# A fused attention unit and token mixer on one core: a square put ahead of the gate, the extra product in full ahead of a group's body, and another order of transposes on SP

## Chip, core and metric

The kernel runs on one core of a Trainium2 chip. The metric is the device time of one execution in microseconds (us), the median of several executions. Five engines run side by side, each through its own list of instructions in order: TensorE (PE in the profile, its weight loads PEld), VectorE (DVE), ScalarE (ACT), GpSimd (POOL) and SyncE (SP), which here only issues transfers. An engine waits on semaphores that other engines or transfers raise.

## Reference

The first stage is a gated attention without a softmax, the second mixes tokens with weights that are made from its own input. In NumPy, with the shapes of this case (8 batches, S = 3200 tokens, D = 256, key width 64):

```python
attn = np.maximum(z @ z.T / S, 0.0) ** 2        # per batch, 3200 x 3200
x = u * (attn @ v)                               # 3200 x 256

wq, wk = x @ w_q, x @ w_k                        # 3200 x 64
W_tok = wq @ wk.T / np.sqrt(64)
mixed = W_tok @ x                                # = wq @ (wk.T @ x) / 8
out = np.maximum(mixed, 0.0) @ w_out             # 3200 x 256
```

`attn` is symmetric, and `W_tok @ x` is computed as `wq @ (wk.T @ x)`, whose inner factor is 64 x 256.

## The kernel before

**Tiles and groups.** The 25 blocks of 128 tokens of a batch make seven groups: six of four blocks (512 tokens) and a last one of a single block. For each of the 8 batches and each group the kernel forms the scores of the group's columns against all blocks, squares them, multiplies them with `v` into two PSUM banks (`acc`), and gates the sum with `u`. A pair of score tiles (128 x 1024) goes through three hands: `scores` (L268) multiplies on PE into one of three rotating PSUM tiles; `first_stage` (L288) clips it at zero into an fp32 tile `g`, on DVE (L293) or ACT (L291); `second_stage` (L298) squares `g` into an fp16 tile `at`, on ACT (L302) or POOL (L304). Since scores are symmetric, many blocks of `at` also serve a later group after a transpose; `second_stage` issues these transposes on SP at once (L321), into tiles `tt`.

**Steps.** The loop of L919 walks through 169 steps. Each computes up to three pairs of scores for later use, squares the three pairs that the step before it clipped (`waiting`), and multiplies a few blocks of the present group with `v` (its body, `second_product`, L423). Scores run two steps ahead of their use (`LAG`). Some pairs of scores are placed ahead of the body (`pairs`, their count is `heading`, L944 to L947), the others between its matmuls (`between_`, placed by `shares`, L863).

**Two lanes.** A body runs with two halves of the PE array side by side: lane LOW contracts rows 0 to 63 into one bank, lane HIGH rows 64 to 127 into the other. Then the lanes change banks, so that each bank gets both halves. `swap_after` (L402) makes PE wait, at that change, for the ends of the matmuls before it.

**Extras.** A step can carry one extra product in its own PSUM tile: a projection of the second stage (`project`, L726), or keys and heads (`keys_and_heads`, L735); the tile comes from the same three rotating ones as the scores. In a step that begins a group, `parts` (L1025 to L1030) is `[extra, banks]`: first halves of the extra, first halves of the body, change, second halves of the extra, change, second halves of the body.

**Gate.** When a group's last step is done, `gate` (L447) reads the two banks: ACT copies the upper one to `gt` (L465), DVE multiplies the lower one with `u` (L466), POOL multiplies `gt` with `u` (L468); a last group of one block has copies on ACT and DVE and an addition and a multiplication on POOL (L458 to L461). The banks are then free for the next group. The result `x_sb` is transposed on SP by `turn_x` (L471) in the next step, after that step's squares and their transposes (L970 to L976).

**Order.** The order on every engine is the order in which the program text issues the instructions; nothing reschedules them. After the loop the last products follow in a fixed order (L1096 to L1140).

Of the kernel before, what the change touches and what calls it, by code (L numbers as in the profile page):

```python
# [10 lines left out]
FP32 = mybir.dt.float32  # L11
RELU = mybir.ActivationFunctionType.Relu
AOP = mybir.AluOpType
# [3 lines left out]
def kernel(  # L17
# [15 lines left out]
    P = 128  # L33
# [40 lines left out]
    def acc_tile(half, name, dtype=FP32):  # L74
# [4 lines left out]
        v0 z00D z01A w10 t0 w2 w1 c0D z10A z11P t1 c1D v1 s0 s1 e0A v2 e1D z20P z21P q0A s2  # L79
        e2D q1A z30P z31P s3 e3A t2 m0 s4 c2D q2A v3 e4D q3P t3 m1 c3D s5 e5A q4A s6 e6D m2  # L80
        s7 e7D
    """
    ctx.enter_context(tc.manual_schedule())

# [213 lines left out]
    def second_stage(p0, g, on_act):  # L298
        at = pat.tile([P, 2 * W], FP16, tag="at", name="at")
        out = at[:].rearrange("p (a w) -> p a w", a=2)  # L300
        if on_act:
            nc.scalar.square(out=out, in_=g[:])  # L302
        else:
            nc.gpsimd.tensor_mul(out=out, in0=g[:], in1=g[:])  # L304
        blocks = []
        for h, (b, gi, tis) in enumerate(tiles[p0 : p0 + 2]):
            for i, ti in enumerate(tis):
                made[b, gi, ti] = (at, h * W + i * widths[gi])
            gj = group_of(tis[0])
            if is_turned(gi, gj):  # L310
                blocks.append((b, gi, gj, tis[0] - starts[gj] // P, 1, h * W, (h + 1) * W))
        if len(blocks) == 2 and blocks[0][:3] == blocks[1][:3] and blocks[1][3] == blocks[0][3] + 1:
            blocks = [blocks[0][:4] + (2, blocks[0][5], blocks[1][6])]
        for b, gi, gj, n0, nn, c0, c1 in blocks:
            if (b, gi, gj) not in turned:
                bufs = {1: 3, 2: 4, 4: 1}[gj - gi]
# [4 lines left out]
            nc.sync.dma_start_transpose(out=out[:, 4 * n0 : 4 * (n0 + nn), :], in_=at[:, c0:c1])  # L321

    accs = {}

# [146 lines left out]
    def turn_x(b, gi):  # L471
        nn = widths[gi] // P
        if gi < LASTG:
            xTs[b, gi] = pxt.tile([P, 4, ND, P], FP16, tag="xT_sb", name="xT_sb")
        else:
            xTs[b, gi] = pxt.tile([P, 1, ND, P], FP16, tag="xTl", name="xTl", bufs=1)
        nc.sync.dma_start_transpose(
            out=xTs[b, gi][:, 0:nn, :, :].rearrange("p n a s -> p (n a) s"),
            in_=xs[b, gi][:, 0:nn, :].rearrange("p n d -> p (n d)"),
        )  # L480
# [392 lines left out]
    def warm(n):  # L873
        if "x" not in begun:
            begun["x"] = acc_tile(1, "sc")
        for _ in range(n):
            nc.tensor.matmul(
                out=begun["x"][:, 0:P], lhsT=zeros[:], rhs=zeros[:], start=True, stop=True
            )

    def opening(order):
        sc, g = {}, {}
        for word in order.split():
            what, n, by = word[0], int(word[1:2]), word[2:]
            if what == "z":
                cast_first(n, int(by[0]), by[1])
            elif what == "t":
                turn_first(n)
            elif what == "c":
                place_first(n, by)  # L890
            elif what == "v":
                load_first_v(*[(0, 4), (12, 6), (18, 7), (4, 8)][n])
            elif what == "s":
                sc[n] = scores(2 * n)
            elif what == "e":
                g[n] = first_stage(2 * n, sc.pop(n), by == "A")
            elif what == "q":
                second_stage(2 * n, g.pop(n), by == "A")
# [17 lines left out]
    across = False  # L916
    left, first_sizes = [], [4, 5, 5, 5]
    gate_pending = False
    while groups:  # L919
        now[0] = k  # L920
        for fn in at_phase.pop(k, []):
# [55 lines left out]
        while asides:  # L977
            asides.pop(0)()

# [38 lines left out]
        if on_lanes:  # L1018
# [13 lines left out]
            emits = []  # L1032
# [4 lines left out]
            cut = len(rows_) // 4  # L1037
            if split:
                emits += both_lanes([bank[:cut] for bank in banks])
            if parts:  # L1040
                across = not across
            for part, ends_ in zip(parts, firsts):
                emits.append((0, lambda ends_=ends_: swap_after(ends_.values())))
                emits += lanes(part, across, True, {})
                if extra and part is extra[0]:
                    emits.append((0, extra[1]))
            if split:
                emits += both_lanes([bank[cut:] for bank in banks])
            at_ = shares(begins, closes, split, len(between_))
            todo = [(x, lambda p0=p0: stage(p0, scores(p0))) for x, p0 in zip(at_, between_)]  # L1050
            for x in acts[1:]:
                todo.append((0.5 - 1e-6, lambda x=x: second_stage(*x)))
            run(emits, todo)
        else:
            assert not is_split(b, gi)
# [11 lines left out]
                    fn()  # L1067
                extra[1]()
            for x in acts[1:]:
                second_stage(*x)  # L1070
            for fn in matmuls[cut:]:
                fn()
        if closes:
# [22 lines left out]
    while to_turn:  # L1096
        turn_x(*to_turn.pop(0))

    def query(gi, o):
        for fn in whole([projections(last, gi, wq2, o)]):  # L1100
            fn()
        projections_out(last, gi, o)

    halves = [(True, nc.sync, 2), (True, nc.sync, 2)]

    psh = ps_tile("hd")
    assert all(kb == last for kb, _ in keyed)
    for fn in whole([heads(last, sum((kgis for _, kgis in keyed), []), psh, stop=False)]):
        fn()
    last_gram(last, LASTG, psg)  # L1110
    g32 = [pg.tile([P, D], FP32, tag="g", name=f"G{cc}") for cc in range(ND)]
    nc.scalar.copy(out=g32[0][:], in_=psg[0])
    nc.vector.tensor_copy(out=g32[1][:], in_=psg[1])
    while len(fillers) > 1:
        mixed = fillers.pop(0)
        proj_out(*mixed, proj(*mixed), [(False, nc.sync, 4)])
    last_heads(last, g32, psh)
    heads_done(last, psh[:, 1, 0:D])
    second = acc_banks("fo")
    proj_half(*fillers[0], second, 0)  # L1120
    query(LASTG - 1, ps_tile("qq")[:, 0, :])
    mixed = [mix(last, 0, db) for db in range(ND)]
    for db in range(ND):
        mix_out(last, 0, db, mixed[db], on_dve=(db == 1))
    proj_half(*fillers[0], second, 1)
    proj_out(*fillers[0], second, halves)
    for db in range(ND):
        mix_out(last, 1, db, mix(last, 1, db))
    query(LASTG, acc_tile(0, "qq")[:, 0:P])
    proj_out(last, 0, proj(last, 0), [(True, nc.sync, 4)])  # L1130
    proj_out(last, 1, proj(last, 1, acc_banks("fo")), halves)
    mix_out(last, 2, 0, mix(last, 2, 0))
    proj_out(last, 2, proj(last, 2), [(True, nc.sync, 4)])
    mix_out(last, 2, 1, mix(last, 2, 1))
    small = acc_banks("mx")
    last_mix(last, small)
    proj_out(last, 3, proj(last, 3), [(True, nc.sync, 4)])
    proj_out(last, 4, proj(last, 4), [(False, nc.sync, 4)])
    proj_out(last, LASTG, proj(last, LASTG), [(False, nc.sync, 1)])
    proj_out(last, 5, proj(last, 5, acc_banks("fo")), [(False, nc.scalar, 2), (True, nc.sync, 2)])  # L1140


# [28 lines left out]
```

## Time and profile before

| | |
|---|---|
| median of 3 executions | 788.06 us (787.47 to 788.28) |
| the profiled execution: its own time | 788.39 us |
| its span, first to last instruction | 786.6 us |
| granted TensorE clock over the span | 0.998 |
| squares on POOL, L304 | 238 of 1.894 us |
| squares on ACT, L302 | 230 of 1.054 us |
| clips on DVE, L293 | 338 of 1.222 us |
| POOL's gate multiply, L468 | 48 of 1.275 us |
| pieces of `at` turned on SP | 162, 5.0 us from issue to landing |

A line of the timeline gives the start in us, the length, the engine, the source line, the operation, the tiles written and read, the shapes, and how many equal instructions in a row were merged (x). Brackets give idle time of the engine ahead of the row and what ended it. Matmul lengths overlap, so the start of one row to the start of the next is the time that PE spent on it.

### The profile page before, as it was taken

The numbers are of one execution on the slowest core, as the hardware profiler recorded it, in microseconds if no ns is written. First come the engines' busy times: TensorE is split into PE (matmuls) and PEld (weight loads), VectorE is DVE, ScalarE is ACT, GpSimd is POOL, SyncE is SP. The second block draws the span as 40 slices with busy tenths as digits, with TensorE's granted clock in tenths as the row PEclk, the third lists the DMA queues.
The fourth block names the chain that finished last, engine by engine and source line by source line (L and its number), as shares of the span: only waits on it lengthen the run. The fifth ranks groups of instructions, "written<-read, shape, count | busy, mean of one in ns | idle before, by whom it ended". The sixth has DMA issues, their size and how long they took to land. (4 is left out here: it accounts for less than half of the span.)

```text
span 786.6 us, 28630 instructions
## 1 busy us (share of the span) xinstructions
PE 770.5 (98%) x12690; PEld 660.9 (84%) x12690; DVE 470.9 (60%) x457; ACT 559.4 (71%) x655; POOL 551.3 (70%) x363
## 2 busy tenths in 40 slices
PE   9999999999999999999999999999999999999996
PEld 6777878887888878889888997898988898988884
DVE  7654666546756567555766557655575646665434
ACT  7666777767768786675867667758696977675464
POOL 7797797667666587765978768885777546866350
PEclk9999999999999999999999999999999999999999
DMA  9999699996999779998799978999589994989626
GB/s 178 179 207 217 124 203 185 194 183 81 245 180 210 175 158 203 195 226 193 171 211 206 236 159 208 200 215 234 123 209 185 244 220 88 198 190 163 159 68 252
DMA packets 276269, 147.06 MB, mean 187 GB/s; under 512 B 252081, under 2 KB 255665, under 8 KB 276145
## 3 DMA queue, kind: packets, MB, share of 16 engines
q1 hardware_dynamic: 275424, 143.33, 88.8%
q0 software_dynamic: 576, 1.64, 1.1%
q8 instruction: 99, 1.62, 0.9%
q14 instruction: 26, 0.20, 0.1%
q10 hardware_dynamic: 144, 0.26, 0.1%
HBM read 59.38 MB, written 26.21 MB: 109 GB/s over the span
## 5 line engine op out<-in xcount | busy, mean ns | idle before, releaser
L293 DVE TENSOR_SCALAR g<-sc 128x1024 f32<-128x1024 f32 x338 | 411.1, 1222 | 260.8 <-PE sc L279 240.4
L337 PE MATMUL acc<-v_sb,at 64*128 64x256 f16 (+1 forms) x7387 | 482.1, 269 | 4.0 <-POOL at L304 1.4
L304 POOL TENSOR_TENSOR at<-g 128x1024 f16<-128x1024 f32 x238 | 445.0, 1894 | 24.2 <-DMA tt<-at 9.0
L337 PEld LDWEIGHTS <-at 64*128 64x128 f16 (+1 forms) x7387 | 388.7, 94 | 68.6 <-PE acc L337 18.1
L302 ACT ACTIVATE at<-g 128x1024 f16<-128x1024 f32 x230 | 237.8, 1054 | 26.8 <-DMA tt<-at 13.2
L468 POOL TENSOR_TENSOR x_sb<-gt,u_sb 128x512 f16<-128x512 f32 x48 | 61.2, 1275 | 181.8 <-ACT gt L465 136.3
L337 PE MATMUL acc<-v_sb,tt 64*128 64x256 f16 (+1 forms) x2540 | 178.5, 269 | 0.0
L279 PE MATMUL sc<-zT 64*128 64x512 f16 (+1 forms) x1104 | 167.6, 344 | 1.4 <-ACT g L291 1.1
L291 ACT ACTIVATE g<-sc 128x1024 f32<-128x1024 f32 x130 | 133.0, 1023 | 37.0 <-PE sc L279 31.7
L337 PEld LDWEIGHTS <-tt 64*128 64x128 f16 (+1 forms) x2540 | 134.8, 94 | 10.2
L279 PEld LDWEIGHTS <-zT 64*128 64x128 f16 x1104 | 60.2, 94 | 9.6 <-issue 3.8
L602 ACT ACTIVATE rt<-mx 128x1024 f16<-128x1024 f32 x47 | 47.8, 1023 | 27.3 <-PE mx L581 25.2
L465 ACT COPY gt<-acc 128x512 f32<-128x512 f32 x48 | 28.1, 585 | 48.6 <-PE acc L337 46.7
L337 PE MATMUL fo<-wo,rt 64*128 64x256 f16 (+1 forms) x688 | 59.5, 269 | 0.8 <-DVE g L293 0.7
L663 ACT ACTIVATE fo<-fo 128x1024 f32<-128x1024 f32 (+2 forms) x44 | 43.6, 998 | 19.8 <-PE fo L337 19.4
L503 ACT CAST qk<-qk 128x512 f16<-128x512 f32 x47 | 27.5, 584 | 40.4 <-PE qk L337 40.1
L337 PE MATMUL qk<-x_sb,kx 64*128 64x256 f16 x368 | 55.1, 269 | 0.9 <-DVE g L293 0.6
L337 PEld LDWEIGHTS <-rt 64*128 64x128 f16 (+1 forms) x688 | 41.3, 94 | 12.8 <-issue 2.4
L466 DVE TENSOR_TENSOR x_sb<-acc,u_sb 128x512 f16<-128x512 f32 x48 | 33.1, 690 | 26.9 <-PE acc L337 24.3
L337 PEld LDWEIGHTS <-kx 64*128 64x128 f16 (+1 forms) x386 | 36.1, 94 | 7.2 <-DMA kx<-qk 0.6
L337 PE MATMUL qk<-xT_sb,wkq 64*128 64x512 f16 (+1 forms) x90 | 31.7, 376 | 0.0
L337 PE MATMUL qk<-xT_sb,wqk 64*128 64x512 f16 (+1 forms) x94 | 30.1, 377 | 0.0
(80 smaller groups left out, 268.5 us busy)
## 6 DMA issues: line engine op xcount, KB each, us to landing
u_sb<-in_u_dram SPq DMA_DIRECT2D x48, 512.0 KB, 5.2
out_dram<-fo SPq DMA_DIRECT2D x45, 512.0 KB, 3.5
piece<-in_v_dram SPq DMA_DIRECT2D x42, 512.0 KB, 4.6
piece<-in_z_dram SPq DMA_DIRECT2D x7, 512.0 KB, 5.8
tt<-at SPq DMA_TRANSPOSE x162, 5.0
piece<-in_z_dram SPq DMA_DIRECT2D x7, 288.0 KB, 5.8
out_dram<-fo SPq DMA_DIRECT2D x5, 256.0 KB, 2.7
u_sb<-in_u_dram SPq DMA_DIRECT2D x8, 128.0 KB, 3.8
```

What stands on the lines that cost most here:

```text
L279: nc.tensor.matmul(out=sc[:, h, at : at + w], lhsT=zT[b][half : half + dqk, ds(z_at(b, h) + ti * P, P)], rhs=zT[b][half : half + dqk, ds(z ...
L291: nc.scalar.activation(out=g[:], in_=sc[:], func=RELU, scale=GSCALE)
L293: nc.vector.tensor_scalar(out=g[:], in0=sc[:], scalar1=0.0, scalar2=GSCALE, op0=AOP.max, op1=AOP.mult)
L302: nc.scalar.square(out=out, in_=g[:])
L304: nc.gpsimd.tensor_mul(out=out, in0=g[:], in1=g[:])
L337: return nc.tensor.matmul(out=self.out, lhsT=self.lhsT(rows), rhs=self.rhs(rows), start=start, stop=stop)
L465: nc.scalar.copy(out=upper[:], in_=accs[1][:])
L466: nc.vector.tensor_mul(out=x[:, 0:n], in0=accs[0][:, 0:n], in1=ug[:, 0:n])
L468: nc.gpsimd.tensor_mul(out=x[:, n : 2 * n], in0=upper[:], in1=ug[:, n : 2 * n])
L503: nc.scalar.copy(out=qks[b, gi][:, 0:gw], in_=out)
L602: nc.scalar.activation(out=out, in_=ps[:], func=RELU)
L663: nc.scalar.mul(out=flat_out[:, sl], in_=part, mul=FINAL_SCALE)
```

## The change

Three things are moved; no matmul and no other operation on data is added or left out.

1. At the end of each group, POOL squares the first of the pairs that the closing step clipped (`staged[0]`) ahead of the gate's own instructions. Before, that square was POOL's first one of the next step, behind the gate multiply. Its transposes are kept back (`ahead`) and issued in the next step.
2. In a step that begins a group with an extra (and whose group isn't the single block run on split lanes), the extra is done in full ahead of the body: its first halves, a change of lanes, its second halves, its output, then the body's two halves with their own change. One pair of scores fewer stands ahead of the body (`heading` falls by two, not by one); two pairs are placed in between, each right in front of one of the two changes of lanes.
3. `second_stage` returns its transposes instead of issuing them. In each step SP now turns `x` first, then the blocks of the first POOL square (`soon`), those of the ACT square, and those of a second POOL square (`late`) only after the body.

The work after the loop is written as a list of words (`ENDING`) that one function reads; its instructions stand in the same order as before.

```diff
@@ second_stage
-        blocks = []
+        blocks, turns = [], []
...
-            nc.sync.dma_start_transpose(out=out[:, 4 * n0 : 4 * (n0 + nn), :], in_=at[:, c0:c1])
+            turns.append(
+                lambda out=out[:, 4 * n0 : 4 * (n0 + nn), :], c0=c0, c1=c1:
+                nc.sync.dma_start_transpose(out=out, in_=at[:, c0:c1])
+            )
+        return turns
...
+    def each(fns):
+        for fn in fns:
+            fn()
@@ the loop over steps
-            heading = heading - bool(keying or projecting) if begins else 1 - bool(mixing)
+            heading = heading - 2 * bool(keying or projecting) if begins else 1 - bool(mixing)
...
-        seconds = [(p0, g, a) for (p0, g), a in zip(waiting, second_on_act)]
+        seconds = [(p0, g, a) for (p0, g), a in zip(waiting, second_on_act) if g is not None]
         acts = [x for x in seconds if x[2]]
-        for x in seconds:
-            if not x[2]:
-                second_stage(*x)
-        for x in acts[:1]:
-            second_stage(*x)
         while to_turn:
             turn_x(*to_turn.pop(0))
+        soon, late = ahead, []
+        for i, x in enumerate([x for x in seconds if not x[2]]):
+            (late if i else soon).extend(second_stage(*x))
+        for x in acts[:1]:
+            each(second_stage(*x))
+        each(soon)
...
+            emits = []
+            apart = extra and begins and not split
+            if apart:
+                turned_ = {}
+                emits += lanes(extra[0], across, False, turned_)
+                first_done = sum(n for n, _ in emits)
+                emits.append((0, lambda: swap_after(turned_.values())))
+                emits += lanes(extra[0], not across, True, {})
+                emits.append((0, extra[1]))
+                parts = [banks]
...
             at_ = shares(begins, closes, split, len(between_))
+            if apart:
+                all_ = sum(n for n, _ in emits)
+                at_ = [(n - 1) / all_ for n in (first_done, halves_, halves_)][: len(between_)]
...
+        each(late)
+        ahead = []
         if closes:
+            if staged:
+                ahead = second_stage(*staged[0], False)
+                staged[0] = (staged[0][0], None)
             gate(b, gi)
...
@@ after the loop
+    ending(ENDING)
```

More of the change, by code (lines that the diff above doesn't have):

```diff
@@ L1039 @@
                 emits += both_lanes([bank[:cut] for bank in banks])
+            halves_ = sum(n for n, _ in emits)
             if parts:
@@ L1044 @@
                 emits += lanes(part, across, True, {})
-                if extra and part is extra[0]:
+                if extra and not apart and part is extra[0]:
                     emits.append((0, extra[1]))
@@ L1069 @@
             for x in acts[1:]:
[L1070 removed]
+                each(second_stage(*x))
             for fn in matmuls[cut:]:
                 fn()
+        each(late)
+        ahead = []
         if closes:
+            if staged:
+                ahead = second_stage(*staged[0], False)
+                staged[0] = (staged[0][0], None)
             gate(b, gi)
@@ L1097 @@
         turn_x(*to_turn.pop(0))
[L1099 to L1140, printed above, removed]
+    assert len(fillers) == 3 and all(kb == last for kb, _ in keyed)
+    ps_, out_, g32 = {}, {}, {}
+    def home(name, where):
+        if where == "a":
+            return acc_banks(name)
+        ps = ps_tile(name)
+        return [ps[:, 0, :], ps[:, 1, :], ps[:].rearrange("p a w -> p (a w)")]
@@ new lines, in ending @@
+    def ending(order):
+        for word in order.split():
+            what, n, more = word[0], int(word[1:2] or 0), word[2:]
+            if what == "H":
+                ps_["hd"] = ps_tile("hd")
+                heads_ = heads(last, sum((kgis for _, kgis in keyed), []), ps_["hd"], stop=False)
+                for fn in whole([heads_]):
+                    fn()
+            elif what == "G":
+                last_gram(last, LASTG, psg)
+            elif what == "g":
+                g32[n] = pg.tile([P, D], FP32, tag="g", name=f"G{n}")
+                (nc.scalar.copy if more == "A" else nc.vector.tensor_copy)(out=g32[n][:], in_=psg[n])
+            elif what == "L":
+                last_heads(last, g32, ps_["hd"])
+            elif what == "h":
+                heads_done(last, ps_["hd"][:, 1, 0:D])
+            elif what == "q":
+                gi = LASTG - 1 + n
+                o = home("qq", more)[0][:, 0 : widths[gi]]
+                for fn in whole([projections(last, gi, wq2, o)]):
+                    fn()
+                projections_out(last, gi, o)
+            elif what == "m":
+                ps_["m", n, more] = mix(last, n, int(more))
+            elif what == "r":
+                db = more[0]
+                mix_out(last, n, int(db), ps_.pop(("m", n, db)), on_dve=(more[1] == "D"))
+            elif what == "s":
+                last_mix(last, home("mx", more))
+            elif what in "fp":
+                which = fillers[n] if what == "f" else (last, n)
+                half = int(more[0])
+                if half == 0:
+                    ps_[what, n] = home("fo", more[1])
+                proj_half(*which, ps_[what, n], half)
+            elif what in "FP":
+                which = fillers[n] if what == "F" else (last, n)
+                key = what.lower(), n
+                if key + ("fo",) not in out_:
+                    out_[key + ("fo",)] = pg.tile([P, 2, W], FP32, tag="g", name="fo")
+                fo = out_[key + ("fo",)][:].rearrange("p a w -> p (a w)")
+                banks_ = ps_[key]
+                at, size, engine, queue = int(more[0]), int(more[1]), more[2], more[3]
+                sl = slice(at * D, (at + size) * D)
+                scale_out(which, at, size, fo[:, sl], banks_, engine, queue)
@@ new lines, in scale_out @@
+    def scale_out(which, at, size, fo, banks_, engine, queue):
+        if at + size <= 2:
+            part = banks_[0][:, ds(at * D, size * D)]
+        elif at >= 2:
+            part = banks_[1][:, ds((at - 2) * D, size * D)]
+        else:
+            part = banks_[2][:, 0 : size * D]
+        if engine == "D":
+            nc.vector.tensor_scalar(
+                out=fo, in0=part, scalar1=FINAL_SCALE, scalar2=None, op0=AOP.mult
+            )
+        else:
+            nc.scalar.mul(out=fo, in_=part, mul=FINAL_SCALE)
+        n0 = starts[which[1]] // P + at
+        (nc.sync if queue == "S" else nc.scalar).dma_start(
+            out=rows(out, which[0])[:, n0 : n0 + size, :],
+            in_=fo.rearrange("p (n d) -> p n d", d=D),
+        )
```

10 lines of the change are left out of this document (7 added, 3 removed).

## Prediction

> **What bounds the kernel.** I read the page first, then PE's waits, then PE's timeline where a group begins, at last the queues of POOL and SP there. The page's first line:
>
> ```profile
> PE 770.5 (98%) x12690; PEld 660.9 (84%) x12690; DVE 470.9 (60%) x457; ACT 559.4 (71%) x655; POOL 551.3 (70%) x363
> ```
>
> PE is busy 98% of the span, every other engine at most 71%. Matmul rows overlap, so this alone proves little: the Trainium skill ("Perfetto Trace Analysis", Identifying the Most-Contended Engine) says that matmul busy time is a bad measure of the distance to the roofline and takes the weight loads' share. By that, 84% here, there would be some 126 us to gain. The starts of matmuls decide. A step that begins a group with an extra, and in which nothing goes wrong:
>
> ```profile
> 505.52 0.59 PE L279 MATMUL sc<-zT 64*128 64x512 f16 x4
> 505.95 0.60 PE L337 MATMUL fo<-wo,rt 64*128 64x256 f16 x8
> 506.46 1.70 PE L337 MATMUL acc<-v_sb,at 64*128 64x256 f16 x28
> ...
> 508.42 0.40 PE L279 MATMUL sc<-zT 64*128 64x512 f16 x2
> 508.63 0.62 PE L337 MATMUL fo<-wo,rt 64*128 64x256 f16 x8
> 509.07 1.71 PE L337 MATMUL acc<-v_sb,at 64*128 64x256 f16 x28
> ```
>
> From 506.46 to 508.42 PE starts 36 matmuls of the body (28, and 8 of the row left out), 0.0544 us each; four score matmuls take 0.43 us (505.52 to 505.95). Laid over the timeline, these rates leave few holes. The eight extras of 505.95 should take 8 x 0.0544 = 0.44 us and take 0.51: the body waits some 0.08 us for the gate to leave the banks. So only holes can be won, as the change neither adds nor removes a matmul. PE's waits name the larger ones:
>
> ```profile
> PE acc L337 <- POOL at L304: 1.4, 2, 0.8
> PE acc L337 <- DVE x_sb L466: 1.2, 4, 0.6
> PE sc L279 <- ACT g L291: 1.1, 2, 0.6
> PE fo L337 <- DVE g L293: 0.7, 1, 0.7
> PE qk L337 <- DVE g L293: 0.6, 1, 0.6
> ```
>
> The timeline shows where they stand:
>
> ```profile
> 100.75 1.27 PE L337 MATMUL acc<-v_sb,at 64*128 64x256 f16 x20 [0.77 <-POOL at L304]
> ...
> 284.40 0.39 PE L337 MATMUL acc<-v_sb,at 64*128 64x256 f16 x4 [0.59 <-POOL at L304]
> ...
> 344.59 1.25 PE L337 MATMUL acc<-v_sb,at 64*128 64x256 f16 x19 [0.58 <-DVE x_sb L466]
> ...
> 474.55 0.61 PE L337 MATMUL fo<-wo,rt 64*128 64x256 f16 x8 [0.74 <-DVE g L293]
> ...
> 692.16 0.28 PE L337 MATMUL qk<-x_sb,kx 64*128 64x256 f16 x1 [0.33 <-DMA kx<-qk]
> ```
>
> The bracket understates a hole, since the last matmul's modelled end still runs into it; I price holes from start to start.
>
> **The square ahead of the gate.** POOL sits idle in front of its gate multiply, because the banks aren't finished:
>
> ```profile
> L468 POOL TENSOR_TENSOR x_sb<-gt,u_sb 128x512 f16<-128x512 f32 x48 | 61.2, 1275 | 181.8 <-ACT gt L465 136.3
> ```
>
> 181.8 / 48 = 3.8 us a gate, against 1.894 us for a square. So the square falls into idle time and all that POOL does until its next idle time comes 1.9 us earlier. PE waits for POOL in two stretches. Near 100: scores at 98.95 take 0.43, eight body matmuls 0.44, so the next was due at 99.82 and came at 100.75: 0.93; some 0.25 more at 105.6. POOL had run without a gap since the gate multiply at 92.37, ahead of which it idled 3.80 us, so both needed squares come 1.9 us earlier. Near 283: 0.3 ahead of 282.55, and 0.8 ahead of 284.40 (eleven matmuls from 283.00 were done by 283.60); here POOL idled 3.72 us before 274.70. All four holes close: **-2.2**, with bounds -2.3 and, if the square itself waits for its `at` tile, -1.1. Cost: by POOL's rows in order of time, 19 of 54 gates have less than 1.9 us idle ahead, and there the gate multiply comes up to 1.9 us later. Behind it on POOL stand casts and squares that the moved square would have delayed anyway; behind it on SP, `turn_x`. The turned `x` is used three steps later or more (L722), some 10 us, so this costs nothing; without that cover it would cost up to 1.9 a group.
>
> **The extra ahead of the body.** By the order of the instructions 37 steps do this. Three effects.
>
> First, the extra's PSUM tile. Scores and extras rotate through three; with one pair of scores fewer in front, the extra takes the tile that the last pair but one of the step before has left. At 474.55 (due at 473.05 + 0.43 = 473.48, a hole of 1.07) the last pair's clip had ended at 474.50, the one before at 473.37. So the extra can run 473.40 to 473.84, and the pair of scores behind it waits until 474.50: 0.66 left, 0.4 won, and 0.2 of the small holes behind it: -0.6. The same at 665.76 (due 664.95): the extra starts on time and takes 0.55, the scores wait for 665.70, -0.4. At 65.30 (hole 0.78, ACT's clip until 65.25) the extra inherits the very tile: 0.
>
> Second, the banks. The body starts later by the extra's second halves, 0.44 us; the second pair of scores still stands ahead of it, only behind the first halves. That covers the 0.08 us hole of an ordinary begin in about 30 steps (-2.3), 0.30 at 154.53, and part of the hole at 344.59 (0.8). There the multiply on DVE waits for `u`, which SP issued some 16 us behind PE: -0.5 if nothing shifts, 0 if SP is as late again by the 1.1 us that PE wins near 283. I take **-0.3 and -0.4**.
>
> Third, the changes of lanes. Before, a change in such a step had other work in front of it and cost nothing: 508.42 to 509.07 is 0.65, just 2 x 0.108 + 8 x 0.0544. Now each has a pair of scores in front. That is what ordinary steps do: scores at 743.28, body at 743.52, 0.24 against 0.21 in the row without a change (740.23 to 740.44): 0.025 each. Two in 37 steps: +1.85. Without that cover one costs far more: at 25.30 there are 62 matmuls in 3.63 us, 3.37 due, so 0.26; all 74 uncovered would be +19, but the order places scores directly ahead of each. Together with the -2.3: **-0.45**.
>
> Scores placed later are clipped up to 0.7 us later; their squares belong to the next step and their use lies two steps ahead, so this hides.
>
> **SP's order.**
>
> ```profile
> 681.31 6.18 SPq L321 DMA_TRANSPOSE tt<-at  x2
> 687.59 1.42 SPq L477 DMA_TRANSPOSE xT_sb<-x_sb  x1
> 689.10 1.53 SPq L510 DMA_TRANSPOSE kx<-qk  x1
> 690.74 1.17 SPq L510 DMA_TRANSPOSE kx<-ql  x1
> ```
>
> The second `tt` of that merged row was issued when POOL's square, begun behind the gate multiply, was done (686.24); `x` and both keys stood behind it. With the square done earlier and `x` first, SP goes on at 684.4 (end of the gate multiply), so the keys come some 1.9 us earlier, and the holes at 692.16 (0.49) and 693.06 (0.36) close: **-0.85**. Blocks of a second POOL square go behind the step's keys and stores; they free `at` tiles (eleven) and feed later groups, so I price this at 0; on the dense stretch it would cost what the slower rival says.
>
> **The ending** keeps its order: 0.
>
> **Sum.** -2.2 - 1.0 - 0.3 - 0.4 - 0.45 - 0.85 = -5.2. The profiled execution took 788.39, 1.8 us of it outside the span and untouched: 783.2. It stands 0.3 above the median of the runs, so I say **783.0**. Its own range, with each term at its bounds, is 780.8 to 785.8.
>
> **Rivals.** *All holes close* (0.14): the openings, the gate waits and changes at no cost, 1.07 + 0.81 + 0.80 + 0.78 + 0.30 + 2.3 + 2.2 + 0.85 = 9.1, so 779.3 at best, 780 as its middle. For it: the changes with scores cost 0.025 at most. Against: DVE's clips at 474.50 and 665.70 don't move.
>
> *The holes only move* (0.14): 787.8. The transfers would set the pace: from 306.39 to 345.89 SP spends 37.3 of 39.5 us on issuing, and what PE wins is lost at the next `u` or `tt`. The Trainium skill ("Perfetto Trace Analysis", What "DMA-bound" means) names an issuing sequencer that is solid with transfers as one form of being bound by them; by it no hole of the stretch would pay. For it: the hole at 344.59. Against: from 378 to 473 the transfer engines' share is 1.00 and PE has hardly a hole.
>
> *Slower through SP* (0.10): `turn_x` now heads SP's queue and waits for a gate multiply that is up to 1.9 us later; SP stands still, and `u` comes late to the next gates. It decides where SP reaches that turn before POOL is done. On the stretch of batches 3 and 4, 12 gates: if half lose 1.9 us to PE, +11 - 5 = +6, so 794. Against: there SP runs over 10 us behind, so the multiply is long done.
>
> **Chances.** Forecast 0.62, all holes 0.14, moved 0.14, slower 0.10. A measurement of this kernel can tell about 0.2% (1.6 us) from no change: faster means below 786.5. The forecast and the first rival lie below, some of the third too: faster 0.79, same 0.12, slower 0.09. The range 780.3 to 787.6 leaves out most of the slower case, half of the best one and part of the moved one, together 0.2.
>
> **What would show it.** Right: no PE wait for POOL near 100 and 283; POOL's idle time ahead of L468 nearly halved; PE's wait for `x_sb` gone; keys on time near 690; 0.2 to 0.24 us for each pair of scores in front of a change. Wrong: PE waits for `tt` or `u_sb`, SP idle ahead of L477, or holes of 0.2 us behind the changes.

## The result, and the profile after

The changed kernel takes **783.52 us**, the median of 6 executions (782.56 to 784.29), against 787.92 for the kernel before beside it (6 executions, 787.40 to 789.16): a ratio of 0.9942, interval 0.9929 to 0.9955. That is 4.4 us less; 783.0 was predicted. The profiled execution of the changed kernel took 782.56 with a span of 780.7, 5.9 less than the span before, at the same granted clock, 0.998.

From the page of the changed kernel: the first line, then POOL's gate multiply (L468 before, L477 now) and POOL's squares (L304 before, L309 now), each with count, busy time and mean, and behind the second bar the idle time ahead of them:

```profile
PE 768.5 (98%) x12690; PEld 627.3 (80%) x12690; DVE 473.5 (61%) x457; ACT 556.9 (71%) x655; POOL 554.9 (71%) x363
L309 POOL TENSOR_TENSOR at<-g 128x1024 f16<-128x1024 f32 x238 | 448.0, 1894 | 122.9 <-DVE g L298 100.1
...
L477 POOL TENSOR_TENSOR x_sb<-gt,u_sb 128x512 f16<-128x512 f32 x48 | 61.2, 1275 | 72.7 <-ACT gt L474 65.3
```

The row of the squares in the kernel before:

```profile
L304 POOL TENSOR_TENSOR at<-g 128x1024 f16<-128x1024 f32 x238 | 445.0, 1894 | 24.2 <-DMA tt<-at 9.0
```

Every engine runs as many instructions as before, and the busy times differ by less than 4 us, except for the weight loads (PEld), which fell from 660.9 to 627.3. What moved is POOL's idle time: ahead of the gates it fell from 181.8 to 72.7 us, and ahead of the squares it rose from 24.2 to 122.9, 100.1 of it waiting for clips on DVE. POOL does no more than before; it idles in front of the moved square rather than behind it, so that square is done before the gate multiply and the next ones start earlier.

From PE's waits in the changed kernel (what waited, for whom, us in total, times, longest):

```profile
PE sc L284 <- ACT g L296: 0.8, 2, 0.6
PE acc L346 <- DVE x_sb L475: 0.7, 4, 0.2
PE sc L284 <- DVE g L298: 0.5, 1, 0.5
```

The rows left out belong to the opening and to the work after the loop, and so does 0.6 of the first row. The waits for POOL's squares (1.4) and for `kx` are gone, the wait for `x_sb` fell from 1.2 to 0.7 and has no long member, and of the two waits of extras for DVE's clip (0.7 and 0.6) one of 0.5 is left, now of a pair of scores. PE's timeline at the places that the prediction named (start, length, operation; PE is 1.0 us earlier behind the hole near 100 and 4.9 us at the keys):

```profile
98.87 0.59 PE L284 MATMUL sc<-zT 64*128 64x512 f16 x4
99.30 1.69 PE L346 MATMUL acc<-v_sb,at 64*128 64x256 f16 x28
100.83 0.38 PE L284 MATMUL sc<-zT 64*128 64x512 f16 x2
...
340.30 0.38 PE L284 MATMUL sc<-zT 64*128 64x512 f16 x2
340.51 0.60 PE L346 MATMUL fo<-wo,rt 64*128 64x256 f16 x8
340.95 0.38 PE L284 MATMUL sc<-zT 64*128 64x512 f16 x2
341.18 0.61 PE L346 MATMUL fo<-wo,rt 64*128 64x256 f16 x8
341.63 1.25 PE L346 MATMUL acc<-v_sb,at 64*128 64x256 f16 x20
...
469.82 0.40 PE L284 MATMUL sc<-zT 64*128 64x512 f16 x2
470.19 0.61 PE L346 MATMUL fo<-wo,rt 64*128 64x256 f16 x8
471.32 0.39 PE L284 MATMUL sc<-zT 64*128 64x512 f16 x2 [0.52 <-DVE g L298]
471.53 0.61 PE L346 MATMUL fo<-wo,rt 64*128 64x256 f16 x8
...
687.23 0.27 PE L346 MATMUL qk<-x_sb,kx 64*128 64x256 f16 x1
```

At 99.30 the 28 matmuls of the body take 1.53 us to the next start, 0.0546 each: the hole is closed. At 340.30 to 341.63 stands the new order: scores, first halves of the extra, scores, second halves, body, each change of lanes behind a pair of scores, and the body no longer waits for the gate. At 470.19 the extra starts 0.15 us late (469.82 and two score matmuls of 0.11 make 470.04), and the second pair of scores waits for the clip in its place. At 687.23 the keys run without a wait.

The keys can start because SP issues their transposes earlier. SP's queue in the changed kernel:

```profile
679.91 1.24 SPq L486 DMA_TRANSPOSE xT_sb<-x_sb  x1
681.20 1.33 SPq L328 DMA_TRANSPOSE tt<-at  x1
682.62 1.21 SPq L519 DMA_TRANSPOSE kx<-qk  x1
683.94 2.15 SPq L519 DMA_TRANSPOSE kx<-ql  x1
```

`x` goes out ahead of the late `tt`. The last key is issued at 683.94, 3.3 us before PE takes the keys; before it was 690.74, 1.4 us before PE started on them at 692.16.

**Where the 5.9 us came from.** For each of the steps I took the time from its first matmul to that of the next step and subtracted what its matmuls need at 0.05433 us for 256 columns on a lane, other widths in proportion. (That is a little under the prediction's 0.0544; with 0.0544 both sums below are 0.95 lower and their difference is the same.) What is left are the step's holes. Where the last matmul of a step ends later than usual behind the start of the next, by up to 0.09 us, the boundary is put later by as much; in the kernel before this is so behind 15 of the 37 begins with an extra in full, where rows of two score matmuls read 0.47 in place of 0.38, and behind none of them in the changed kernel. The ends are modelled, so this choice is a reading: it moves holes between neighbouring steps, but not their sum. Over all steps the holes sum to 20.42 us before and 14.67 after, a difference of 5.75 out of the 5.9 of the span:

| place (start of the step before, us) | before | after | won | predicted |
|---|---|---|---|---|
| square ahead: 98.95, 103.62, 282.02 | 2.41 | 0.10 | 2.31 | 2.2 |
| extra's PSUM tile: 473.05 | 1.56 | 0.87 | 0.69 | 0.6 |
| extra's PSUM tile: 664.52 | 0.88 | 0.41 | 0.47 | 0.4 |
| extra's PSUM tile: 64.30 | 1.05 | 0.34 | 0.71 | 0 |
| banks: 153.36 | 0.34 | 0.07 | 0.27 | 0.3 |
| banks: 342.83 | 0.90 | 0.18 | 0.72 | 0.4 |
| the other 33 begins with an extra in full | 2.93 | 2.18 | 0.75 | 0.45 |
| keys: 690.69 | 0.97 | 0.01 | 0.96 | 0.85 |
| five begins of a single-block group with an extra | 0.36 | 1.41 | -1.05 | none |
| all others | 9.01 | 9.11 | -0.10 | 0 |

The row of the 33 begins hangs on that choice: counted from first start to first start alone they go from 1.78 to 2.23 us, and the gain stands in the steps behind them. The last row but one is a loss that the prediction didn't have.

### The profile page after: what moved, and what is told of

It is laid out like the page before. It is cut to its first block, busy times and chain, and to the rows that moved or that the text cites. A ratio compares the mean times of both kernels' runs of the same rounds, so it can differ in the third digit from the quotient of the medians.

```text
span 780.7 us, 28613 instructions
## 1 busy us (share of the span) xinstructions
PE 768.5 (98%) x12690; PEld 627.3 (80%) x12690; DVE 473.5 (61%) x457; ACT 556.9 (71%) x655; POOL 554.9 (71%) x363
## 5 line engine op out<-in xcount | busy, mean ns | idle before, releaser
L309 POOL TENSOR_TENSOR at<-g 128x1024 f16<-128x1024 f32 x238 | 448.0, 1894 | 122.9 <-DVE g L298 100.1
L346 PE MATMUL acc<-v_sb,at 64*128 64x256 f16 (+1 forms) x7387 | 474.5, 269 | 1.8 <-DVE x_sb L475 0.7
L346 PEld LDWEIGHTS <-at 64*128 64x128 f16 (+1 forms) x7387 | 364.9, 94 | 87.4 <-PE acc L346 25.0
L346 PE MATMUL acc<-v_sb,tt 64*128 64x256 f16 (+1 forms) x2540 | 174.8, 269 | 0.0
L346 PEld LDWEIGHTS <-tt 64*128 64x128 f16 (+1 forms) x2540 | 127.2, 94 | 15.0
L477 POOL TENSOR_TENSOR x_sb<-gt,u_sb 128x512 f16<-128x512 f32 x48 | 61.2, 1275 | 72.7 <-ACT gt L474 65.3
L284 PEld LDWEIGHTS <-zT 64*128 64x128 f16 x1104 | 55.5, 94 | 11.2 <-issue 3.9
L512 ACT CAST qk<-qk 128x512 f16<-128x512 f32 x47 | 27.5, 586 | 37.3 <-PE qk L346 37.2
L346 PEld LDWEIGHTS <-rt 64*128 64x128 f16 (+1 forms) x688 | 35.9, 94 | 15.2 <-PE fo L346 5.1
L672 ACT ACTIVATE fo<-fo 128x1024 f32<-128x1024 f32 x39 | 39.9, 1024 | 4.3 <-PE fo L346 4.3
```

What stands on the lines that cost most here:

```text
L284: nc.tensor.matmul(out=sc[:, h, at : at + w], lhsT=zT[b][half : half + dqk, ds(z_at(b, h) + ti * P, P)], rhs=zT[b][half : half + dqk, ds(z ...
L346: return nc.tensor.matmul(out=self.out, lhsT=self.lhsT(rows), rhs=self.rhs(rows), start=start, stop=stop)
L477: nc.gpsimd.tensor_mul(out=x[:, n : 2 * n], in0=upper[:], in1=ug[:, n : 2 * n])
L512: nc.scalar.copy(out=qks[b, gi][:, 0:gw], in_=out)
L672: nc.scalar.mul(out=flat_out[:, sl], in_=part, mul=FINAL_SCALE)
```

## The experiments

The kernels ran in three jobs; each is compared with the kernel before of its own job: 788.02 (23 executions, 787.03 to 791.70), 788.32 (9, 788.01 to 788.76) and 788.11 (11, 787.02 to 792.23). "Holes" is the count above over all steps but four, those that start at 37.3, 50.7, 64.3 and 145.0 in the kernel before: the first and the last two change from one execution to the next (last section); 50.7 is left out with them, though it only goes from 0.25 to 0.32 where `heading` falls by two. Without them it is 18.51 us before and 13.30 after.

| kernel | parts of the change | median (range) | ratio (interval) | holes |
|---|---|---|---|---|
| e1 | 1 | 784.35 (783.71 to 785.12) | 0.9941 (0.9922 to 0.9959) | 14.66 |
| e2 | 2 | 788.24 (787.20 to 792.53) | 1.0003 (0.9987 to 1.002) | 19.15 |
| e3 | 3 | 788.24 (786.01 to 791.07) | 0.9994 (0.9977 to 1.001) | 17.24 |
| e11 | 1, 3 | 783.13 (782.70 to 785.43) | 0.9937 (0.9916 to 0.9957) | 14.18 |
| e5 | 1, 2, 3: the change again | 784.03 (783.00 to 785.77) | 0.9949 (0.9936 to 0.9962) | 13.20 |
| e4 | 1, 2 mended, 3 | 782.77 (782.42 to 785.19) | 0.9924 (0.9903 to 0.9946) | 12.23 |
| e6 | as e4 | 781.96 (781.30 to 783.15) | 0.9922 (0.9910 to 0.9935) | 12.13 |
| e9 | as e4 | 783.03 (781.95 to 785.38) | 0.9933 (0.9913 to 0.9953) | 12.14 |
| e7 | 1, 2 mended | 782.98 (781.81 to 783.51) | 0.9930 (0.9917 to 0.9944) | 12.56 |
| e10 | as e7 | 782.37 (781.90 to 783.78) | 0.9923 (0.9903 to 0.9943) | 12.39 |
| e8 | 1, 2 with a change uncovered, 3 | 790.57 (790.10 to 792.08) | 1.0033 (1.0020 to 1.0045) | 21.83 |

**Part 1 alone.** The kernel before, with the first POOL square of the next step put ahead of the gate; its transposes stay at the head of the step's, and `x` behind them.

```diff
+        each(ahead)
         for x in seconds:
             if not x[2]:
-                second_stage(*x)
+                each(second_stage(*x))
...
         if closes:
+            if staged:
+                ahead = second_stage(*staged[0], False)
+                staged[0] = (staged[0][0], None)
             gate(b, gi)
```

> Only part 1 of the change: POOL squares the first pair of the closing step ahead of the gate; the extra and SP's order are as before (the transposes of that square are issued first in the next step, then the others, then x). My theory, that the parts act on separate holes: the four holes behind POOL near 100, 105, 282 and 284 us close (-2.2), and the keys near 690 also come earlier, because the transpose that held SP no longer waits for a square behind the gate multiply (-0.85); the hole at 65.3 us stays. 784.9 to 785.2 against 787.9 before, ratio 0.9963. Rival, that the extra's place makes the gain and POOL only stops being seen: 787.5 or more.

It took 784.35 (ratio 0.9941), 3.7 us less than the kernel before of its job: most of the gain comes from this part, more than was expected. From PE's waits in it:

```profile
PE fo L341 <- DVE g L293: 0.7, 1, 0.7
PE qk L341 <- DVE g L293: 0.6, 1, 0.6
```

No row names POOL's squares (the one row that names POOL, 0.4 us, is of a cast in the opening), and the two waits for the extra's tile stand as before. The three steps near 100 and 282 fell to 0.03, 0.03 and 0.02 us of holes. Two further things closed. The keys at 690.69 fell from 0.97 to 0.01 with SP's order untouched: with the square done earlier, the second `tt` no longer holds up the queue. The merged row of the two `tt` that took 6.18 us in the kernel before, and the last key behind it:

```profile
677.98 4.19 SPq L323 DMA_TRANSPOSE tt<-at  x2
...
684.93 1.90 SPq L514 DMA_TRANSPOSE kx<-ql  x1
```

And 473.05 fell from 1.56 to 1.15. There the extra still waits for its tile (0.74), but the body behind it starts on time (472.08, the extra at 471.65), where it was 0.18 late before (475.17, the extra at 474.55), and the 0.33 of holes inside the body's first halves are gone; what ended those was not followed. In the kernel before, the copy that frees one of the banks had itself waited for POOL, as DVE's timeline shows:

```profile
474.69 0.42 DVE L459 COPY gt<-acc 128x256 f32<-128x256 f32 x1 [0.20 <-POOL at L304]
```

**Part 2 alone.** The kernel before, with the extra in full ahead of the body and `heading` less two.

```diff
-            heading = heading - bool(keying or projecting) if begins else 1 - bool(mixing)
+            heading = heading - 2 * bool(keying or projecting) if begins else 1 - bool(mixing)
...
+            apart = extra and begins and not split
+            if apart:
...
+                parts = [banks]
```

> Only part 2: the extra in full ahead of the body, one pair of scores fewer in front, squares and SP as before. My theory: holes at 344, 474, 665 and 154 us shrink (0.7 + 0.6 + 0.45 + 0.27), ordinary begins win 0.45, and the five begins of a single-block group with an extra lose 0.2 each (+1.05), since the fewer scores in front no longer cover the gate: about -1.4, so 786.5, ratio 0.9982; the holes behind POOL near 100 and 283 us stay. Rival, that the extra's place is the main part: 784 or less.

788.24, ratio 1.0003: it gained nothing, where 786.5 was expected. At the begins it did what was foreseen: the 37 with an extra in full went from 6.61 us of holes to 4.37, and the five of a single-block group lost 1.05. But PE then also met POOL earlier, at squares that hadn't moved. From PE's waits in this kernel, where the first row stood at 1.4 before:

```profile
PE acc L337 <- POOL at L304: 2.5, 4, 1.0
...
PE qk L337 <- DMA kx<-ql: 0.5, 1, 0.5
PE qk L337 <- DMA kx<-qk: 0.4, 1, 0.4
```

And two places of PE's timeline:

```profile
283.90 0.83 PE L337 MATMUL acc<-v_sb,at 64*128 64x256 f16 x12 [1.02 <-POOL at L304]
...
383.53 0.61 PE L337 MATMUL acc<-v_sb,at 64*128 64x256 f16 x8 [0.69 <-POOL at L304]
```

The step at 282.02 grew from 1.10 to 1.63 us of holes, the one at 381.78 from 0.01 to 0.87, the keys from 0.97 to 1.35; 98.95 fell by 0.21. So of the 2.24 won, 1.05 goes to the part's own loss at the single-block begins, and the rest, and more, comes back at squares on POOL and at the keys. For that rest the rival "the holes only move" is what happens, though what paces PE is POOL at two of the three places, and not the transfers that the prediction named.

**Part 3 alone.** The kernel before, with SP's order changed.

```diff
+        while to_turn:
+            turn_x(*to_turn.pop(0))
+        soon, late = [], []
+        for i, x in enumerate([x for x in seconds if not x[2]]):
+            (late if i else soon).extend(second_stage(*x))
...
+        each(late)
```

> Only part 3: SP turns x first and the blocks of a second POOL square after the body; squares and extra as before. My theory: SP no longer waits for the square behind the gate multiply, the keys near 690 us come 1.5 us earlier and that hole closes (-0.85), all else stays: 787.0, ratio 0.9989. Rival, that blocks at the end of SP's order come too late and free their tiles later: 788.5 or more, with PE or POOL waiting for tt.

788.24, ratio 0.9994, and in the profile the keys' hole is gone (0.01). So SP's order closes it too, as the prediction had it; but part 1 closes it without that. PE still waits for POOL:

```profile
PE acc L341 <- POOL at L304: 1.4, 2, 0.8
```

The gain of 1.27 in the profile's holes (0.96 at the keys, 0.28 at 342.83) doesn't show in the median, where 787.0 was expected: the executions of this kernel spread over 5 us. Three of the twelve ran at a granted clock of 0.995 or 0.996 and took 789.75 to 791.07; the other nine have a median of 786.87, against 787.94 for the 21 executions of the kernel before at 0.997 or more. That agrees with the holes, but the choice was made afterwards and the nine spread over 2.8 us, so it is a hint and no more.

**The begins of a single block.** The changed kernel takes two pairs of scores out of the front of every begin with an extra, but puts the extra in full ahead of the body only where the group isn't the single block. In the five begins of such a block that carry an extra, one pair fewer is left to cover the gate, and nothing is won for it. Two early begins, at 50.72 and 64.30, lose a pair in the same way: their extra runs on the whole array and isn't put apart either. The first went from 0.25 to 0.32 us of holes; at the second the scatter hides it. The mend leaves these two alone and keeps `heading` as it was for the five:

```diff
-            heading = heading - 2 * bool(keying or projecting) if begins else 1 - bool(mixing)
+            heading = heading - (2 - is_split(*groups[0])) * bool(keying or projecting) if begins else 1 - bool(mixing)
```

> The changed kernel, but a step that begins a single-block group on split lanes with an extra keeps two pairs of scores in front, as before the change. My theory: the five holes of 0.2 us that the change opened there, where the body waits for the gate, close: -1.05 against the changed kernel's 783.5, so 782.5, ratio 0.9929 to before. Rival, that these holes come from the change of lanes losing its scores, or merely move to the next step: no gain, 783.5.

> The same kernel as e4_split_heading, to settle its distance from the changed kernel on one chip: 782.5 to 782.8, so 0.7 to 1.0 us below e5_changed_again, if the five holes of 0.2 us are real and do not come back later; the same time as e5_changed_again by the rival that they move.

> The kernel of e6_split_again once more, as the measure of the next two: 782.0 to 782.8.

PE's timeline at such a begin, first in the changed kernel, then in e6:

```profile
91.19 0.38 PE L284 MATMUL sc<-zT 64*128 64x512 f16 x2
91.41 0.38 PE L346 MATMUL qk<-xT_sb,wqk 64*128 64x512 f16 x1
...
92.13 0.83 PE L346 MATMUL acc<-v_sb,at 64*128 64x256 f16 x12
```

```profile
90.93 0.60 PE L284 MATMUL sc<-zT 64*128 64x512 f16 x4
91.36 0.38 PE L346 MATMUL qk<-xT_sb,wqk 64*128 64x512 f16 x1
...
91.87 0.83 PE L346 MATMUL acc<-v_sb,at 64*128 64x256 f16 x12
```

From the first score to the body both take 0.94 us, with one pair in the changed kernel and two in e6: the gate sets the body's start, and the pair taken out is 0.22 us that PE stands idle. The five fell from 0.31, 0.20, 0.24, 0.35 and 0.31 us of holes to 0.09, 0.01, 0.03, 0.13 and 0.10 in e4, and to the same within 0.01 in e6 and e9: 1.04 us. The medians are 782.77, 781.96 and 783.03, below the changed kernel's 783.52 and 784.03: by 2.1 in the one job that held both (e5 and e6), more than was expected. The size is the profile's; the times only agree in sign.

> The changed kernel as it is, beside the next two on the same chip. 783.5 as before, ratio 0.9942.

The changed kernel repeated: 784.03, holes 13.20 against 13.30.

**The mended kernel without SP's order.** e4 with `x` turned last again and no blocks kept for later:

```diff
-        while to_turn:
-            turn_x(*to_turn.pop(0))
-        soon, late = ahead, []
-        for i, x in enumerate([x for x in seconds if not x[2]]):
-            (late if i else soon).extend(second_stage(*x))
+        each(ahead)
+        for x in seconds:
+            if not x[2]:
+                each(second_stage(*x))
...
-        each(late)
```

> e6_split_again without part 3: SP turns the blocks of all squares first and x last, as before the change. My theory after e1 and e3: with the square ahead of the gate SP no longer waits for it in either order, so the order is worth nothing: the same time as e6_split_again, within 0.4 us, and the keys near 686 us still on time. Rival, that x and the keys need SP's new order: 0.85 more or worse.

> The kernel of e7_without_sp_order once more. Two readings of its 1.0 us over e6 are open. If SP's new order is worth something by itself, the median lies 0.8 to 1.2 over e9_split_third again. If the difference was the scatter of the holes near 37 and 64 us, which come and go from one execution to the next, what stays is the one hole that both profiles without the order show near 465 us: 0.25, so 0 to 0.5 over e9_split_third.

782.98 and 782.37, against 781.96 and 783.03 for the mended kernel with SP's order in the same jobs: 1.0 above in one job, outside the 0.4 that was expected, and 0.7 below in the other, so the times don't show whether the order is worth anything. In the holes one step tells them apart, the begin at 468.73, which has 0.56 in e7 and e10 and 0.32 in e6 and e9. The keys' step has 0.05 and 0.01 without the order. The prediction's 0.85 for it is not its own: either of two parts wins it.

**A change of lanes without cover.** The changed kernel with both pairs of scores in front of the body's change, so that the extra's change has none:

```diff
-                at_ = [(n - 1) / all_ for n in (first_done, halves_, halves_)][: len(between_)]
+                at_ = [(n - 1) / all_ for n in (halves_, halves_, halves_)][: len(between_)]
```

> The changed kernel, but in the 37 steps with the extra in full both pairs of scores stand in front of the second change of lanes and none in front of the first. My theory: an uncovered change costs what it does in other steps, 0.25 us, against 0.03 with scores in front: 37 x 0.22 = +8, so 791.5, ratio 1.0045, each such step longer by 0.2 with the hole between the extra's halves. Rival, that the first change costs nothing because the extra writes PSUM banks of its own: 783.5.

790.57, 6.5 us above the changed kernel of its job (784.03) and slower than the kernel before. The begin that the prediction showed at 505.52, in this kernel and then in the changed one:

```profile
507.08 0.38 PE L284 MATMUL sc<-zT 64*128 64x512 f16 x2
507.30 1.28 PE L346 MATMUL fo<-wo,rt 64*128 64x256 f16 x16
508.41 1.69 PE L346 MATMUL acc<-v_sb,at 64*128 64x256 f16 x28
```

```profile
501.77 0.60 PE L346 MATMUL fo<-wo,rt 64*128 64x256 f16 x8
502.21 0.38 PE L284 MATMUL sc<-zT 64*128 64x512 f16 x2
502.44 0.61 PE L346 MATMUL fo<-wo,rt 64*128 64x256 f16 x8
502.89 1.69 PE L346 MATMUL acc<-v_sb,at 64*128 64x256 f16 x28
```

The sixteen extras need 0.87 us and take 1.11 uncovered: 0.24 for the change. With a pair of scores in it the same stretch takes 1.12, and 0.22 of that is the pair's own work. So the uncovered change costs 0.24, the covered one about 0.03. The step has 0.256 us of holes instead of 0.061; the 37 begins sum to 10.91 instead of 3.64, and two later steps (381.78 and 573.30) add 0.56 each.

**Parts 1 and 3 without 2.** The changed kernel with the old `heading` and the extra never apart:

```diff
-            heading = heading - 2 * bool(keying or projecting) if begins else 1 - bool(mixing)
+            heading = heading - bool(keying or projecting) if begins else 1 - bool(mixing)
...
-            apart = extra and begins and not split
+            apart = False
```

> Parts 1 and 3 without part 2 (the extra and the scores in front as before). If part 2 makes its gain only beside the square ahead of the gate, this takes what e1 took or 0.25 less, 784.1 to 784.4, ratio 0.9948, and part 2 with two scores in front of the split begins is worth 1.7 to 2.0; the gate holes of 0.08 us and those at 474 and 665 us are back. Rival: part 2 is worth nothing in any company, as in e2, and this takes 782.5.

783.13, against 783.03 for the mended kernel e9 in the same job; 784.1 to 784.4 was expected. The times don't separate them, so they don't rule out the rival either. The profiled executions are alike too, with spans of 780.84 and 780.81, because e9's opening took 1.6 us longer; inside the loop e11 needs 1.6 us more. There the holes separate them: PE's wait of 0.7 for the extra's tile is back at

```profile
470.49 0.61 PE L346 MATMUL fo<-wo,rt 64*128 64x256 f16 x8 [0.74 <-DVE g L298]
```

and the holes sum to 14.18 against 13.30 and 13.20 with part 2 as written and 12.14 (e9) with it mended. By the holes part 2 is worth 0.9 to 1.0 beside parts 1 and 3, and 2.0 with the single-block begins mended. Whether a median of many executions would show that was not settled.

## Why the prediction came out

**The square ahead of the gate (-2.2): right.** 2.31 won at the three steps, and e1 wins the same by itself. The idle time ahead of the gate multiply was to be nearly halved and fell by 60%, because POOL now waits for DVE's clip ahead of the moved square. The hidden costs stayed hidden: no PE wait for `tt` or `u_sb` came up.

**The extra's PSUM tile (-1.0): the mechanism right, the credit in part wrong.** 1.16 was won at the two steps priced, and what is left there is a pair of scores waiting for DVE's clip, as worked out. At 664.52 the 0.47 is part 2's, since e11 still has 0.88 there. At 473.05 part 1 alone wins 0.41 of the 0.69, in the body; part 2 beside it wins 0.27 (1.15 in e11), not 0.6. At 64.30 the prediction had 0 and the profiled execution shows 0.71, but that step isn't evidence: it lies between 0.26 and 1.87 in the thirteen profiles.

**The banks (-0.3 and -0.4): the amount right at 153.36 (0.27), too small at 342.83 (0.72).** At 153.36 part 1 alone wins 0.21 of it. At 342.83 the gain lies beyond the outer end of 0.5, because more happened than "nothing shifts": DVE's multiply no longer waits for `u`. Its row before, and in the changed kernel:

```profile
343.85 0.69 DVE L466 TENSOR_TENSOR x_sb<-acc,u_sb 128x512 f16<-128x512 f32 x1 [1.48 <-DMA u_sb<-in_u_dram]
```

```profile
340.53 0.69 DVE L475 TENSOR_TENSOR x_sb<-acc,u_sb 128x512 f16<-128x512 f32 x1 [0.70 <-PE acc L346]
```

SP issued that `u` 4.9 us ahead of the multiply before (338.91) and 8.9 us ahead in the changed kernel (331.59). The wait is gone in e1, e2 and e3 as well, so it can't be credited to one part; why SP is further ahead there, and whether every execution of the kernel before has the wait, stays open. Without part 2 0.61 us of holes remain (e11), with part 2 alone 0.18 (e2), so the 0.44 that the body starts later is part 2's. The Trainium skill ("Perfetto Trace Analysis", What "DMA-bound" means) counts a kernel whose issuing sequencer is solid with transfers as bound by them; by it no hole of that stretch would pay. The measurement differs: the 0.72 was won where SP had been issuing 37.3 of 39.5 us (36.8 of 39.5 in the changed kernel), and the next hole of such a kind, 0.87 at 381.78 in e2, was POOL's and is 0.01 in the changed kernel.

**Ordinary begins and changes of lanes (-0.45): right in kind, 0.75** over the 33 begins that had no price of their own, with the boundaries of steps as chosen above. Those with some 0.1 us of holes came down to about 0.06, and the few that had had 0.01 to 0.02 rose to between 0.05 and 0.09: two covered changes at 0.025 to 0.03 each are what is left. The 0.26 read for an uncovered change was 0.24 in e8, where the cover was taken away.

**The step that failed: the heading.** The prediction costs "one pair of scores fewer in front" only for the 37 steps that do the extra in full. The diff lowers `heading` in every begin with an extra, in 44 steps: the 37, the five of a single block, where the pair had been the gate's cover (+1.05 us, unpriced), and the two on the whole array (+0.07 at 50.72). The instruction order showed those steps; I had counted only the 37.

**SP's order (-0.85): the amount right (0.96), the cause too narrow.** The prediction's own sentence named both "the square done earlier and `x` first"; the sum gave it all to the order. Either closes it. Of the rival "slower through SP" one sign came: SP's waits ahead of turning `x` add up to 85 us, against 52 before. But no wait of PE for `tt` or `u_sb` came of it.

**The rivals.** "The holes only move" is the fate of much of part 2 alone (e2) and not of the whole: what it wins at its begins stays won only once POOL's square has moved. All holes closing was ruled out where it was to be: the clips on DVE still hold 0.87 and 0.41.

**The sum.** The terms missed by +1.05 for the single-block begins and by amounts between 0.1 and 0.7 the other way, which all but cancelled: -5.75 of holes in the profiles for -5.2. That the median fell by 4.4 and not by 5.8 lies within what executions of one kernel scatter: the profiled execution is the quickest of its six. So the prediction came out closer than its parts were, and that is luck: 0.71 of what offset the forgotten steps is the scatter at 64.30, and 0.3 is the `u` that came earlier than was assumed.

On the weight loads' share: by that measure of the Trainium skill ("Perfetto Trace Analysis", Identifying the Most-Contended Engine) alone, the distance to the roofline would have grown, as the share fell from 84% to 80% (153 us without a weight load after, 126 before) in a kernel that got faster. The Trainium skill names the share of the peak rate (MFU) beside it, which rises when the same matmuls take less time. The starts of matmuls leave 14.7 us of holes.

## What to carry to other kernels

Where PE is near its bound, count holes from start to start, step by step, and do it for every step that a shared count such as `heading` reaches, also those where the rest of the edit doesn't apply: a pair of matmuls taken from the front of a wait costs its full length there. An edit that makes PE ready earlier pays only if what it meets next is ready earlier too: the extra's new place alone gained nothing, since PE ran into POOL's squares (and lost 1.05 us at the single-block begins), and beside the moved square its begins paid in the holes, though no median shows it by itself. One pair of score matmuls in front of a change of lanes brought its cost from 0.24 us to 0.03, so place the filler exactly there.

## What was unexpected

Executions of one kernel differ by up to 3 us or so at one granted clock (0.997 to 0.999): e4's six ran from 782.42 to 785.19. The profiles put the difference into a few early steps and into the opening, whose instructions are the same in every kernel: the loop's first matmul comes at 11.96 us in one profile and at 13.73 in another. In e4's profiled execution, of 785.19 us, the step that starts at 64.3 in the kernel before has 1.87 us of holes, and the steps at 37.3 and 145.0 have 1.36 and 1.38; in e6, which is the same kernel at 781.30, they have 0.34, 0.57 and 0.04. ACT's timeline of e4, and PE's behind it:

```profile
64.41 1.06 ACT L307 ACTIVATE at<-g 128x1024 f16<-128x1024 f32 x1 [3.34 <-DMA tt<-at]
65.38 1.03 ACT L146 CAST v_sb<-piece 128x1024 f16<-128x1024 f32 x1
66.31 1.01 ACT L296 ACTIVATE g<-sc 128x1024 f32<-128x1024 f32 x1
```

```profile
65.41 0.38 PE L284 MATMUL sc<-zT 64*128 64x512 f16 x2
67.38 0.59 PE L346 MATMUL qk<-xT_sb,wkq 128*128 128x512 f16 x2 [1.58 <-ACT g L296]
```

ACT's square waits for the transfer that frees its `at` tile; the cast and the clip stand behind it on ACT, and PE's extra waits for the clip. In the changed kernel's profile the same square starts at 61.57, the clip at 63.47. At 37.3 ACT's square waits for such a transfer too (4.91 us); at 145.0 PE waits for DVE (1.17), which waits for a cast on ACT, in whose queue a square had waited 2.40 for one. So how late that transfer lands seems to differ from one execution to the next, at the same place of the same kernel; what makes it late was not followed. This is also why differences of 1 us between two medians of six could not be told here, while single holes of 0.2 us could.
